# Asking for the copy of the turned shift rows two steps, not three, behind its transposing transfer

## The chip, the cores and the metric

One core of a Trainium2 chip runs the whole program. The metric is the device time of one execution in microseconds. A core has TensorE (matrix products), VectorE, ScalarE, GpSimd (POOL in the profile), and SyncE (SP), which here does nothing but issue transfers. The profile calls a transfer's issue by its queue, SPq for SyncE's.

## The reference

Three stages follow each other. Clustered attention lets a query attend only to keys of its own cluster; then comes a dense layer with a maximum over three products, and last a layer of eight experts. The change lies in the attention.

```python
q_assign = np.argmax(np.einsum('bhsd,hcd->bhsc', q_n, c_n), axis=-1)
k_assign = np.argmax(np.einsum('bhsd,hcd->bhsc', k_n, c_n), axis=-1)
mask = q_assign[:, :, :, None] == k_assign[:, :, None, :]
scores = np.where(mask, scale * np.matmul(q, k.transpose(0, 1, 3, 2)), -1000000000.0)
scores = scores - np.max(scores, axis=-1, keepdims=True)
attn = np.exp(scores)
attn = attn / (np.sum(attn, axis=-1, keepdims=True) + 1e-09)
attn_out = np.matmul(attn, v)                      # 2 batches, 8 heads, 768 rows, 64 wide
h = np.maximum(np.maximum(x @ w1, x @ w2), x @ w3) # x: 1536 rows of 512
x = h @ w_out
# then each row with x @ w_skip > 0 goes through one of 8 experts, weighted by its gate
```

## The kernel before

The 16 heads (two batches of eight) go through in pairs. This text numbers them 0 to 15; a pair holds an even head, called first, and an odd one, called second. A head takes six steps of the loop in `attention`, one for each tile of 128 keys, so there are 96 steps, and some before them to fill the pipeline. Each step asks every engine for a fixed list of instructions: two score products of two parts each (line 524, tiles Aq, Ak, Cq, Ck), the exponentials on ScalarE (line 527), the products with the values (line 565) of two steps before, and one step of the row maximum of a head that is up to eleven steps ahead (lines 465, 470 and 475).

The row maximum of a head has to be subtracted from its scores. The kernel does that inside the score product: the plane Aq holds, beside the query rows, 32 rows of shift values for each head. `shift` makes them when the head's sixth maximum is done: three small operations of GpSimd write the tile mq (lines 489 to 494), SyncE issues a transposing transfer from mq into a tile named pm (line 512), and later a second transfer copies 32 rows of pm into Aq (line 543). For heads 0 and 1 TensorE turns the rows instead, and ScalarE copies them. So the profile has 14 transposing transfers into pm and 14 copies out of it, in the order of heads 2 to 15. The first score product of a head (line 524) needs its copy.

`later(n, fn)` calls fn when the loop is n steps on, at the beginning of that step. What a step asks for is issued in the order of the calls, and each engine runs its own list in order. The transfers of SyncE thus stand in one list: a transfer whose source isn't there yet holds all that follow it. In that list stand also the loads of raw keys and queries (rawk, rawq, line 306), of the values (v, line 409) and of the dense layer's weights (wst and wsto, line 743), the copies of the key and query halves (Ak, Aq, Ck, Cq, lines 327 and 333), the transposed cluster rows (Mk, Mq, lines 512 and 543) and the transposed results (xh, xl, lines 611 and 615). The weights' loads have two buffers, and VectorE frees one when it has read it.

The copy's place is set by these lines; PW is a number in the table CF.

```python
M = self.turned(f"pm{nm}", mq.rearrange("p n j c -> p (n j c)"))
self.later(PW, lambda: self.copies()[AW[st["b"]]](Aq[r, j, :], M[r]))
```

AW is 2 for both batches, which picks SyncE's transfer as the copy.

Of the kernel before, what the change touches and what calls it, by code (L numbers as in the profile page):

```python
# [79 lines left out]
 'QS': 2,  # L80
 'QT': 6,
 'MW': [2, 0, 0],
 'PW': 3,
 'XS': 3,
 'XL': 1,
 'XR': [0, 1, 2],
# [1417 lines left out]
```

## Time and profile before

| | |
|---|---|
| time before, median of 3 executions | 526.34 us (525.97, 526.34 and 529.37) |
| the profiled execution | 530.19 us |
| its span, first to last instruction | 528.4 us |
| TensorE busy, products | 480.8 us (91%) |
| TensorE, loading of weights | 330.1 us (62%) |
| VectorE busy | 391.2 us (74%) |
| ScalarE busy | 314.0 us (59%) |
| GpSimd busy | 152.7 us (29%) |
| mean granted clock of TensorE | 0.970 |

Busy times come from one profiled execution. The loading of weights overlaps with the products. The granted clock is a share of TensorE's full speed. The attention's steps take the time from about 30 us to 320 us; up to about 145 us of it the attention runs nearly alone, and from there the dense layer's work is woven in.

### The profile page before, as it was taken

How to read it: one execution, taken by the hardware profiler on the slowest of the kernel's cores; microseconds unless marked ns; L12 is line 12 of the kernel's file. 1: busy time of each engine (PE TensorE's matmuls, PEld its weight loads, DVE VectorE, ACT ScalarE, POOL GpSimd, SP SyncE). 2: the span in 40 equal slices, each digit the busy share in tenths (PEclk: the TensorE clock that was granted, in tenths of full speed). 3: DMA queues.
4: the chain of work that ended last, by engine and by line, in shares of the span. 5: the costliest groups of instructions: out<-in, count | busy, mean ns of one | idle time of the engine just before them, and what ended most of it. 6: DMA issues, size and time to landing. Idle time of an engine off the chain costs nothing. (4 is left out here: it accounts for less than half of the span.)

```text
span 528.4 us, 11560 instructions
## 1 busy us (share of the span) xinstructions
PE 480.8 (91%) x4390; PEld 330.1 (62%) x4390; DVE 391.2 (74%) x828; ACT 314.0 (59%) x579; POOL 152.7 (29%) x197
## 2 busy tenths in 40 slices
PE   2689999899897989899999999999999999977993
PEld 1357777677775767566776766655656654445763
DVE  5656676645689899999999973344588867588992
ACT  5587777567676675656666654311556633465980
POOL 2424242422438344745375320000000000271112
PEclk9999999969998999989999999999999999989898
DMA  8649486935849427744534125316488854299970
GB/s 229 156 118 219 92 182 111 227 76 119 177 103 244 92 93 178 152 107 128 134 71 115 66 44 96 71 41 248 151 276 261 267 178 155 80 302 291 358 256 14
DMA packets 89836, 82.91 MB, mean 157 GB/s; under 512 B 55200, under 2 KB 72806, under 8 KB 89778
## 3 DMA queue, kind: packets, MB, share of 16 engines
q1 hardware_dynamic: 88082, 78.98, 55.5%
q0 software_dynamic: 976, 1.85, 1.7%
q10 hardware_dynamic: 720, 1.31, 0.7%
q8 instruction: 35, 0.57, 0.5%
q14 instruction: 23, 0.19, 0.1%
HBM read 57.18 MB, written 4.22 MB: 116 GB/s over the span
## 5 line engine op out<-in xcount | busy, mean ns | idle before, releaser
L527 ACT ACTIVATE p<-p 128x384 f32<-128x384 f32 x192 | 92.4, 492 | 53.4 <-PE p L524 48.5
L841 PE MATMUL h<-xh,wh 128*128 128x384 f16 x288 | 94.9, 330 | 1.8 <-DVE xl L604 1.8
L841 PE MATMUL h<-xh,wl 128*128 128x384 f16 x288 | 95.2, 330 | 0.0
L841 PE MATMUL h<-xl,wh 128*128 128x384 f16 x288 | 95.0, 330 | 0.0
L565 PEld LDWEIGHTS acc<-v,p 128*128 128x128 f32 x672 | 84.6, 197 | 9.1 <-issue 3.8
L565 PE MATMUL acc<-v,p 128*128 128x65 f32 x672 | 84.2, 276 | 0.3
L475 DVE CUSTOM_DVE_ANT_0 mh<-p,mh 128x384 f32<-128x384 f32 x96 | 52.9, 551 | 33.8 <-ACT mh L470 24.8
L841 PEld LDWEIGHTS <-wh 128*128 128x128 f16 x576 | 55.6, 100 | 35.5 <-DVE xl L604 1.9
L1108 DVE SCALAR_TENSOR_TENSOR e<-est,e 128x1024 f16<-128x1024 f32 x64 | 76.6, 1218 | 0.9 <-ACT e L1105 0.9
L524 PE MATMUL p<-Aq,Ak 128*128 128x384 f16 x192 | 64.7, 337 | 6.9 <-DMA Aq<-pm 3.4
L1105 ACT ACTIVATE e<-est 128x1024 f16<-128x1024 f32 x64 | 65.0, 1049 | 6.2 <-DMA est<-in_moe_w 5.6
L524 PE MATMUL p<-Cq,Ck 128*128 128x384 f16 x192 | 64.6, 336 | 0.0
L768 POOL TENSOR_TENSOR wma<-wma,wpw 128x512 f32<-128x512 f32 x24 | 31.3, 1306 | 66.4 <-DVE wma L767 44.2
L470 ACT ACTIVATE mh<-p 128x384 f32<-128x384 f32 x96 | 46.7, 487 | 2.8 <-PE p L465 2.4
L849 DVE TENSOR_TENSOR hm<-h,hm 128x384 f32<-128x384 f32 x48 | 26.6, 555 | 27.1 <-PE h L841 25.0
L854 ACT ACTIVATE hh<-hm 128x384 f16<-128x384 f32 x24 | 12.6, 523 | 55.7 <-DVE hm L849 55.7
L538 DVE TENSOR_TENSOR pl<-p,ph 128x768 f16<-128x768 f32 x40 | 42.5, 1062 | 2.6 <-ACT ph L537 2.6
L1147 POOL DMA_INDIRECT exe<-out,ixe x2 | 2.2, 1084 | 141.6 <-DVE me L1143 141.3
L841 PEld LDWEIGHTS <-wl 128*128 128x128 f16 x288 | 28.4, 99 | 19.2 <-issue 0.8
L465 PE MATMUL p<-Ak,Aq 128*128 128x384 f16 x96 | 33.7, 351 | 6.3 <-DVE mx L475 4.2
L465 PE MATMUL p<-D,Aq 128*128 128x384 f16 x96 | 33.9, 353 | 1.8 <-DVE D L338 1.6
L537 ACT ACTIVATE ph<-p 128x768 f16<-128x768 f32 x40 | 33.7, 844 | 1.3
(234 smaller groups left out, 916.0 us busy)
## 6 DMA issues: line engine op xcount, KB each, us to landing
est<-in_moe_w SPq DMA_DIRECT2D x64, 512.0 KB
wst<-in_moe_w SPq DMA_DIRECT2D x18, 512.0 KB
rawk<-in_kT SPq DMA_DIRECT2D x8, 384.0 KB
rawq<-in_qT SPq DMA_DIRECT2D x8, 384.0 KB
v<-in_vP SPq DMA_DIRECT2D x16, 192.0 KB
wsto<-in_moe_w_out SPq DMA_DIRECT2D x6, 512.0 KB
Ak<-Hk SPq DMA_DIRECT2D x16, 96.0 KB
Aq<-Hq SPq DMA_DIRECT2D x16, 96.0 KB
```

What stands on the lines that cost most here:

```text
L465: nc.tensor.matmul(pb[:, :384], lhsT=Aq[:, j, 128 * n:128 * n + 128], rhs=(st["D", j], Ak[:, j, 384:768])[u], start=True, stop=True)
L470: nc.scalar.activation(pbs[0], pb[:, :384], AF.Relu)
L475: nc.vector.tensor_tensor_reduce(pbs[0], pbs[1][:, :384], pbs[0], 1.0, -3.0e38, ALU.add, ALU.max, mx[:, n:n + 1])
L524: nc.tensor.matmul(pb[:, :384], lhsT=T["k"][:, j, ks], rhs=T["q"][:, j, 384 * u:384 * u + 384], start=first, stop=not first)
L527: nc.scalar.activation(p[:, u], pb[:, :384], AF.Exp, scale=2.0 ** -19)
L537: nc.scalar.activation(ph, p, AF.Copy)
L538: self.low_p = lambda: nc.vector.tensor_tensor(plo, p, ph, op=ALU.subtract)
L565: nc.tensor.matmul(o, lhsT=l, rhs=r, start=start, stop=stop, skip_group_check=True)
L768: nc.gpsimd.tensor_tensor(ma[i], ma[i], pw[i].bitcast(F32), op=ALU.mult)
L841: nc.tensor.matmul(ps[:, :384], lhsT=l, rhs=r[:, k, :], start=(k == 0 and i == 0), stop=(k == self.NK - 1 and i == 2))
L1105: nc.scalar.activation(hi, st, AF.Copy, scale=64.0)
L1108: nc.vector.scalar_tensor_tensor(lo, st, 64.0, hi, op0=ALU.mult, op1=ALU.subtract)
```

## The change

The number of steps between asking for the transposing transfer and asking for the copy goes from three to two. Nothing else is touched; every engine has the same instructions as before.

```diff
  'MW': [2, 0, 0],
- 'PW': 3,
+ 'PW': 2,
  'XS': 3,
```

On SyncE this moves the copy up in the list. Two places show it. The first is in the list of SyncE at the copy for head 4, the first head of its pair; Mk and Mq are the turned cluster rows of the next pair. Before:

```order
L512 DMA_TRANSPOSE pm_2_0_1261<-mq 128x6x128
L512 DMA_TRANSPOSE Mq_3_1297<-aq 128x6x128
L543 DMA Ak_3_1177<-Mk_3_1254 64x768 x2
L543 DMA Aq_3_1180<-Mq_3_1297 64x768 x2
L543 DMA Aq_2_674<-pm_2_0_1261 32x768
L327 DMA Ck_0_1488<-Lk_0_1380 64x768 x2
```

The same place of SyncE's list, with the change:

```order
L512 DMA_TRANSPOSE pm_2_0_1261<-mq 128x6x128
L512 DMA_TRANSPOSE Mq_3_1297<-aq 128x6x128
L543 DMA Ak_3_1177<-Mk_3_1254 64x768 x2
L543 DMA Aq_2_674<-pm_2_0_1261 32x768
L543 DMA Aq_3_1180<-Mq_3_1297 64x768 x2
```

The copy has changed places with the two copies of the next pair's turned query rows.

The second place is SyncE's list at the copy for head 5, the second head of the same pair; wst is a load of the dense layer's weights. Before:

```order
L512 DMA_TRANSPOSE pm_2_1_1498<-mq 128x6x128
L409 DMA v_3_1560<-in_vP 128x6x64 x2
L327 DMA Cq_0_1582<-Hq_0_1378 64x768 x2
L327 DMA Cq_0_1582<-Lq_0_1443 64x768 x2
L306 DMA rawk_1_1628<-in_kT 128x768
L306 DMA rawq_1_1630<-in_qT 128x768
L743 DMA wst_0_1633<-in_moe_w 128x4x256
L543 DMA Aq_2_674<-pm_2_1_1498 32x768
L611 DMA_TRANSPOSE xh_122<-x_1_1_1637 128x6x128
```

The same place of SyncE's list, with the change:

```order
L327 DMA Cq_0_1582<-Lq_0_1443 64x768 x2
L543 DMA Aq_2_674<-pm_2_1_1498 32x768
L306 DMA rawk_1_1629<-in_kT 128x768
L306 DMA rawq_1_1631<-in_qT 128x768
L743 DMA wst_0_1634<-in_moe_w 128x4x256
L611 DMA_TRANSPOSE xh_122<-x_1_1_1637 128x6x128
```

The copy now stands ahead of the loads of raw keys, raw queries and weights. For heads 3 and 7 it passes rawk and rawq alone. For head 11 it passes a load of weights alone, for head 14 a load of the last weights (wsto), and for heads 13 and 15 its place in SyncE's list stays as it was.

## Rows read from the trace of the kernel before

**Rows 1.** The page, busy time of each engine with its share of the span.
```profile
PE 480.8 (91%) x4390; PEld 330.1 (62%) x4390; DVE 391.2 (74%) x828; ACT 314.0 (59%) x579; POOL 152.7 (29%) x197
```

**Rows 2.** Waits from 60 to 320 us: us in total, times, longest.
```profile
PE p L465 <- DVE mx L475: 4.2, 4, 1.5
...
PE p L524 <- DMA Aq<-pm: 3.4, 2, 1.9
```

**Rows 3.** Timeline of TensorE at heads 4, 5, 7: start, us, instruction, idle before.
```profile
86.44 0.10 PEld L524 LDWEIGHTS <-Ak 128*128 128x128 f16 x1
...
102.56 0.34 PE L524 MATMUL p<-Aq,Ak 128*128 128x384 f16 x1 [1.95 <-DMA Aq<-pm]
...
136.40 0.34 PE L524 MATMUL p<-Aq,Ak 128*128 128x384 f16 x1 [1.48 <-DMA Aq<-pm]
```

**Rows 4.** Timeline of SyncE's issues, for heads 5, 7 and 15.
```profile
89.63 2.20 SPq L512 DMA_TRANSPOSE pm<-mq  x1
...
95.89 0.58 SPq L306 DMA_DIRECT2D rawk<-in_kT  x1
...
97.48 0.57 SPq L543 DMA_DIRECT2D Aq<-pm  x1
...
129.95 0.58 SPq L306 DMA_DIRECT2D rawk<-in_kT  x1
...
131.06 0.57 SPq L543 DMA_DIRECT2D Aq<-pm  x1
...
302.50 1.25 SPq L512 DMA_TRANSPOSE pm<-mq  x1
305.37 0.53 SPq L543 DMA_DIRECT2D Aq<-pm  x1
```

**Rows 5.** Timeline of SyncE's issues, for head 4.
```profile
77.48 1.89 SPq L512 DMA_TRANSPOSE pm<-mq  x1
...
80.80 1.23 SPq L543 DMA_DIRECT2D Ak<-Mk  x2
...
84.52 0.55 SPq L543 DMA_DIRECT2D Aq<-pm  x1
```

**Rows 6.** Waits of SyncE itself at line 543, whole span.
```profile
SPq L543 <- DMA Mq<-aq: 2.1, 4, 1.2
SPq L543 <- DMA pm<-mq: 1.6, 1, 1.6
```

**Rows 7.** Timelines of ScalarE and VectorE around 100 us.
```profile
99.99 0.52 ACT L527 ACTIVATE p<-p 128x384 f32<-128x384 f32 x1
103.09 0.49 ACT L527 ACTIVATE p<-p 128x384 f32<-128x384 f32 x1 [2.58 <-PE p L524]
...
101.08 0.55 DVE L475 CUSTOM_DVE_ANT_0 mh<-p,mh 128x384 f32<-128x384 f32 x1
```

**Rows 8.** Stretches: us, busy PE, PEld, DVE, ACT, POOL; PEclk, DMA, GB/s.
```profile
100.00:102.00 2.00, 0.61 (x19) 0.49 (x17) 1.64 (x4) 0.51 (x2) 1.05 (x2) 1.00 1.14 326
102.00:104.00 2.00, 1.44 (x10) 1.12 (x10) 0.00 (x1) 0.91 (x3) 1.84 (x4) 0.92 1.12 239
104.00:112.00 8.00, 8.00 (x38) 6.56 (x38) 2.44 (x8) 3.18 (x6) 3.36 (x5) 0.50 1.00 138
112.00:114.00 2.00, 2.00 (x9) 1.45 (x8) 1.97 (x5) 1.62 (x4) 0.65 (x1) 0.52 0.31 76
...
134.00:137.00 3.00, 1.52 (x25) 1.08 (x23) 1.95 (x6) 0.89 (x4) 1.66 (x3) 1.00 1.21 136
```

**Rows 9.** Timeline of TensorE: last products of heads 1, 3, 5 and 7.
```profile
63.30 0.35 PE L565 MATMUL acc<-vs,Aq 32*128 32x65 f16 x6
...
91.52 0.35 PE L565 MATMUL acc<-vs,Aq 32*128 32x65 f16 x6
...
125.88 0.36 PE L565 MATMUL acc<-vs,Aq 32*128 32x65 f16 x6
...
155.00 0.35 PE L565 MATMUL acc<-vs,Aq 32*128 32x65 f16 x6
```

## The prediction

> **What bounds the kernel now.** I read the busy shares first, then the waits of TensorE, then the queue of SyncE around those waits, and last the granted clock. TensorE is busy for 91% of the span [rows 1]. So the kernel is as long as TensorE's fixed list of instructions plus the holes in it, and a hole that is closed early moves all the later work forward, since each engine's instructions stand in a fixed order and the later loads are asked for by the same steps. The list of waits names few holes. One of them is the copy of this change: TensorE waits twice for the transfer of the shift rows into the query plane (the tile Aq, from pm), 3.4 us in total [rows 2]. The two places are the first score product of head 5, at 102.56 us after 1.95 us of idling, and of head 7, at 136.40 us after 1.48 us [rows 3]. The other twelve copies landed before TensorE was there or cost it almost nothing.
>
> The queue tells why these two. SyncE issued the transposing transfer of head 5 at 89.63 us and the copy out of its result only at 97.48, behind the loads of the next raw keys and queries and a load of weights (rawk, rawq, wst; 384, 384 and 512 KB), which took its place from 95.89 on; for head 7 the copy went out at 131.06, behind rawk and rawq from 129.95 on [rows 4]. From issue to the product it took 102.56 - 97.48 = 5.08 us and 136.40 - 131.06 = 5.34 us. A copy of head 4, which has no big loads ahead of it, was issued at 84.52 [rows 5], and TensorE loaded weights for that head's first product at 86.44 [rows 3]: at most 1.92 us. So the copy is late for two reasons: it is asked for late, and it rides behind big loads.
>
> **The change part by part.** Nothing is added or removed; a copy moves up one step, past what SyncE issues in that step. There are two kinds of place.
>
> *Second head of a pair (heads 3, 5, 7, 9 and 11).* The copy moves ahead of rawk, rawq or a load of weights, or all of them. Head 5's copy takes rawk's place, 95.89, and head 7's takes 129.95. What does its landing become? Both ends come from rows: at best 1.92 us after issue (97.81 and 131.87), at worst as long as before (95.89 + 5.08 = 100.97 and 129.95 + 5.34 = 135.29), since the four copies Cq and the values v still stand ahead. TensorE would have been ready at 102.56 - 1.95 = 100.61 and at 136.40 - 1.48 = 134.92. The rest of the wait is 0 to 0.36 us at head 5 and 0 to 0.37 at head 7. The gain is 1.59 to 1.95 plus 1.11 to 1.48, together 2.7 to 3.4 us. I take 3.4: what made 5.1 out of 1.9 must be mostly the megabyte that no longer stands ahead.
>
> *First head of a pair (heads 2, 4, 6, ...).* The copy now stands between Ak<-Mk and Aq<-Mq (heads 2 to 12). TensorE waited for none of these, so the gain is nought. The cost could be that SyncE stands at the copy until the transposition lands. The copy's new place in head 4's pair is 80.80 + 1.23 = 82.03 us, 4.55 us after its transposition was issued [rows 5]. The one transposition whose landing SyncE did wait for, at 302.50 us, was followed by its copy 2.87 us later [rows 4], and SyncE's waits list that single wait, of 1.6 us [rows 6]. So the new place comes late enough, and I take nought; behind the copy stand the two Aq<-Mq, which wait for a transposition issued later anyway. Were that cover gone, they would be later by the missing time plus the copy's own 0.55 us of issue.
>
> *What is moved past.* rawk, rawq and wst go out 0.57 us later, the issue time of the copy [rows 4]. The waits of 60 to 320 us, of which two stand in [rows 2], hold none of any engine for these three. So nought again, and at most 0.57 us a pair if the cover were gone.
>
> *What is late next.* At head 5, ScalarE had ended its last exponential at 99.99 + 0.52 = 100.51 and then sat idle 2.58 us waiting for TensorE; VectorE's row maximum of that step ended at about 101.6 [rows 7]. TensorE's next need of ScalarE was thus met 0.1 us before 100.61, and it needs that maximum's bank only in the next step. Nothing takes the wait's place at once.
>
> *The sum.* Against the profiled execution (530.19 us: a span of 528.4 and 1.8 us around it): 530.19 - 3.4 = 526.8 us. Against the median, 526.34 - 3.4 = 522.9 us.
>
> **The clock.** There is a second price on head 5's wait. After it the granted clock fell: 1.00 in 100 to 102 us, 0.92 in 102 to 104, 0.50 in 104 to 112, 0.52 in 112 to 114 [rows 8]: the lower of two levels (1.2 against 2.4 GHz) for about 0.3 + 8 + 1.9 = 10.2 us. Head 7's shorter wait left the clock at 1.00 [rows 8]. What did it cost? The last products of a head mark a period. Two heads take 91.52 - 63.30 = 28.22 us before, 155.00 - 125.88 = 29.12 after, which holds the wait of 1.48 (so 27.64), and 125.88 - 91.52 = 34.36 over the slow stretch, which holds the wait of 1.95 [rows 9]. The excess is 34.36 - 1.95 - 28.22 = 4.2 to 34.36 - 1.95 - 27.64 = 4.8 us; I use 4.5. In the profiled execution this goes too if the wait goes: 526.8 - 4.5 = 522.3. But the profiled execution is 3.85 us above the median, and of the three times two lie at 526 and one at 529.37. A slow stretch of 4.5 us that comes in some executions and not in others would explain that split. So I hold it likelier that the median execution had the wait without the fall of the clock, and has only 3.4 us to win.
>
> The Trainium skill ("TensorE: Matmul & The Clock Gate", section "HAM oscillation — how this bites in real kernels") prices a slow stretch at its length times one half. By that it would be worth 10.2 x 0.5 = 5.1 us, and the rival below with the clock would end 0.6 us lower; the periods say 4.2 to 4.8, and the sum goes by them.
>
> **The rivals.** *The clock comes back too:* the median execution had the slow stretch like the profiled one, and without the wait it doesn't come. 526.34 - 3.4 - 4.5 = 518.4 us. For it speaks that the clock fell right behind the longest wait; against it that one of two waits had no such effect, and that the profile is slower than the median. *The wait is given back:* the copy lands early, but TensorE, now up to 3.4 us ahead, meets another hole: the list has waits for VectorE's maximum, 4.2 us in four [rows 2]. If they grow by what is won, the time stays at 526.3. Against it speaks that VectorE and ScalarE idle in the stretch of the two waits [rows 7]. The same time comes out if the copy lands no sooner in spite of its new place, but the bound above leaves that only 0.7 us. *Slower:* SyncE stands at the copy in its new place, because under load the transposition takes longer than the 4.55 us that separate them. SyncE's longest wait of that kind, for another transposition (Mq), is 1.2 us [rows 6]. At the seven first heads this is up to 8.4 us of a stopped queue; if the keys and queries behind it passed all of it on to TensorE, 526.34 - 3.4 + 8.4 = 531.3 us. It decides from a landing later than 4.55 us after issue, for which no row speaks.
>
> **How the numbers follow.** The waits alone go: 522.9, chance 0.50. The clock too: 518.4, 0.25. Given back: 526.3, 0.17. Slower: 531.3, 0.08. The forecast is 522.9. The range leaves out the slower case and the lower part of the clock's: 518.0 to 526.8. One per cent is 5.3 us, about what a measurement of this kernel can tell from no change. Faster by more than that needs less than 521.1: nearly all of the clock's case (0.24) and a fifth or so of the first, where a part of the slow stretch goes as well (0.11), together 0.35. Slower by that much, above 531.6, is the upper half of the last case and what I may have overlooked: 0.06. Within one per cent: 0.59.
>
> **What would show it.** Right: in the waits of TensorE the entry for this copy shrinks from 3.4 us to below 0.8; the copies of heads 5 and 7 leave SyncE ahead of rawk; two heads take about 28 us also between the marks that now lie 34.36 apart. The clock of that stretch shows whether the second price is gone, and a fall elsewhere that it has moved. Wrong: SyncE's wait for the transposition grows well over 1.6 us (the slower rival), or TensorE's waits for VectorE or ScalarE grow by about 3 us between 100 and 300 us (given back). What would break the forecast most is the clock, since it costs more than both waits and doesn't follow from the order of instructions.

## The result, and the profile after

The changed kernel takes 521.76 us in the median of six executions (516.35 to 525.84); before takes 526.63 us, also of six (524.96 to 529.37). The ratio is 0.9888, with a 95% interval of 0.9842 to 0.9933. The profiled execution took 519.58 us, with a span of 517.8 us. A repetition on another chip, told below, gives 521.41 against 527.01 us.

The ratios leave out executions more than 1.5% above the fastest of their kernel, for before 13 of 29 in the second set below and 10 of 23 in the third, so that a ratio there tends to understate a gain, and the medians of all executions stand beside it.

The list of waits from 60 to 320 us, of the changed kernel (us in total, times, longest us), no longer has TensorE's entry for the copy that [rows 2] show:

```profile
PE p L465 <- DVE mx L475: 5.3, 6, 1.5
...
PE h L841 <- DVE xl L604: 2.5, 1, 2.5
...
PE p L524 <- ACT p L527: 1.6, 5, 0.5
```

The timeline of TensorE shows the first score products of heads 5 and 7 without idle time before them, where [rows 3] had 1.95 and 1.48 us, and the last products of heads 1, 3, 5 and 7, as in [rows 9], and of head 15:

```profile
62.19 0.35 PE L565 MATMUL acc<-vs,Aq 32*128 32x65 f16 x6
...
90.16 0.35 PE L565 MATMUL acc<-vs,Aq 32*128 32x65 f16 x6
...
99.04 0.33 PE L524 MATMUL p<-Aq,Ak 128*128 128x384 f16 x1
...
117.81 0.35 PE L565 MATMUL acc<-vs,Aq 32*128 32x65 f16 x6
...
126.70 0.33 PE L524 MATMUL p<-Aq,Ak 128*128 128x384 f16 x1
...
145.28 0.36 PE L565 MATMUL acc<-vs,Aq 32*128 32x65 f16 x6
...
330.87 0.35 PE L565 MATMUL acc<-vs,Aq 32*128 32x65 f16 x6
```

Two heads now take 27.97, 27.65 and 27.47 us; before they took 28.22, 34.36 and 29.12. From the mark of head 1 to that of head 7 the profiled executions differ by 91.70 - 83.09 = 8.6 us, of a difference in span of 528.4 - 517.8 = 10.6. So four fifths of the difference lie in these three pairs. Of the 8.6 us, 3.4 are the two waits, and most of the rest is the slow stretch behind head 5, which this execution of before had and another one (below) had not.

SyncE's timeline shows where the copies went (compare [rows 4, 5]); the first three rows are head 4's, the next three head 5's, the last two head 7's:

```profile
79.44 1.28 SPq L543 DMA_DIRECT2D Ak<-Mk  x2
80.83 0.56 SPq L543 DMA_DIRECT2D Aq<-pm  x1
82.03 1.11 SPq L543 DMA_DIRECT2D Aq<-Mq  x2
...
94.47 0.56 SPq L543 DMA_DIRECT2D Aq<-pm  x1
95.08 0.58 SPq L306 DMA_DIRECT2D rawk<-in_kT  x1
...
96.23 0.38 SPq L743 DMA_DIRECT2D wst<-in_moe_w  x1
...
122.15 0.56 SPq L543 DMA_DIRECT2D Aq<-pm  x1
122.76 0.58 SPq L306 DMA_DIRECT2D rawk<-in_kT  x1
```

Head 5's copy went out 4.57 us before the product that needs it, head 7's 4.55 us, and neither held TensorE. The list of transfers (KB each, median us from issue to landing) shows that the fourteen copies were not all as quick as the 1.92 us of the prediction's better end:

```profile
Aq<-pm SPq DMA_DIRECT2D x14, 48.0 KB, 3.3
```

SyncE's own waits at line 543 for the transposition are 2.4 us in two, at heads 14 and 15, against one of 1.6 before [rows 6]:

```profile
SPq L543 <- DMA pm<-mq: 2.4, 2, 1.5
```

The granted clock (PEclk, the third number from the end, ahead of DMA share and GB/s) stays at 1.00 behind head 5, where [rows 8] had 0.50. The one fall of the clock in the attention came later, behind a stretch in which TensorE was busy for 2.06 us of 5:

```profile
100.00:102.00 2.00, 2.00 (x19) 1.74 (x18) 1.41 (x5) 0.82 (x3) 1.80 (x3) 1.00 1.20 204
102.00:110.00 8.00, 8.00 (x80) 6.57 (x78) 5.12 (x14) 7.09 (x15) 3.06 (x6) 1.00 1.09 164
...
155.00:160.00 5.00, 2.06 (x26) 1.42 (x26) 4.97 (x11) 1.61 (x4) 3.58 (x5) 0.97 1.01 287
160.00:164.00 4.00, 4.00 (x19) 2.25 (x17) 3.96 (x6) 2.58 (x6) 3.32 (x4) 0.61 1.02 167
```

It isn't head 5's fall in a new place: before had a fall of the same length there, about 3.4 us at the lower level, beside the one behind head 5. Before:

```profile
165.00:168.00 3.00, 1.01 (x20) 0.78 (x20) 3.00 (x7) 1.37 (x3) 2.01 (x3) 1.00 1.06 294
168.00:172.00 4.00, 4.00 (x16) 1.90 (x15) 4.00 (x7) 1.30 (x3) 3.57 (x4) 0.57 0.87 203
```

### The profile page after: what moved, and what is told of

Its sections match the earlier page's. It is cut to its first block, busy times and chain, and to the rows that moved or that the text cites. A ratio compares the mean times of both kernels' runs of the same rounds, so it can differ in the third digit from the quotient of the medians.

```text
span 517.8 us, 11568 instructions
## 1 busy us (share of the span) xinstructions
PE 470.1 (91%) x4390; PEld 324.3 (63%) x4390; DVE 393.6 (76%) x828; ACT 313.5 (61%) x579; POOL 154.7 (30%) x197
## 5 line engine op out<-in xcount | busy, mean ns | idle before, releaser
L565 PEld LDWEIGHTS acc<-v,p 128*128 128x128 f32 x672 | 81.7, 192 | 9.6 <-issue 4.4
L565 PE MATMUL acc<-v,p 128*128 128x65 f32 x672 | 81.7, 271 | 0.2
L524 PE MATMUL p<-Aq,Ak 128*128 128x384 f16 x192 | 63.0, 328 | 3.9 <-ACT p L527 1.8
L524 PE MATMUL p<-Cq,Ck 128*128 128x384 f16 x192 | 62.8, 327 | 0.0
L538 DVE TENSOR_TENSOR pl<-p,ph 128x768 f16<-128x768 f32 x40 | 44.0, 1101 | 2.6 <-ACT ph L537 2.6
L465 PE MATMUL p<-Ak,Aq 128*128 128x384 f16 x96 | 32.5, 339 | 8.1 <-DVE mx L475 5.3
L465 PE MATMUL p<-D,Aq 128*128 128x384 f16 x96 | 32.7, 341 | 1.8 <-DVE D L338 1.6
```

The lines of the kernel that those rows point to most:

```text
L465: nc.tensor.matmul(pb[:, :384], lhsT=Aq[:, j, 128 * n:128 * n + 128], rhs=(st["D", j], Ak[:, j, 384:768])[u], start=True, stop=True)
L524: nc.tensor.matmul(pb[:, :384], lhsT=T["k"][:, j, ks], rhs=T["q"][:, j, 384 * u:384 * u + 384], start=first, stop=not first)
L538: self.low_p = lambda: nc.vector.tensor_tensor(plo, p, ph, op=ALU.subtract)
L565: nc.tensor.matmul(o, lhsT=l, rhs=r, start=start, stop=stop, skip_group_check=True)
```

## The experiments

The theory: the gain is the copy of heads 5 and 7 that no longer stands behind the big loads in SyncE's list; its price is the two waits and, in executions where the clock falls behind head 5's wait, that fall. The rivals: the first heads' copies have a part, the number of steps matters and not the order, or the gain is chance in the clock. Three sets ran, each on one chip with its own executions of before: 27 (median 527.94 us, mean granted clock 0.9757), 29 (526.51 us, 0.9787) and 23 (527.01 us, 0.9771).

### First set: which copies, and is it the order?

**Second heads alone.** The copies of heads 3, 5, 7, 9, 11, 13 and 15 two steps behind, the others three.

```diff
- self.later(PW, lambda: ...
+ self.later(PW - j, lambda: ...
```

> Only the second heads of the pairs (3, 5, 7, 9, 11) get the copy two steps behind; the first heads keep three. My theory (the gain is the copy put ahead of the raw loads at heads 5 and 7): like the changed kernel, no wait of TensorE for this copy above 0.4 us in total, granted clock 1.00 behind head 5, ratio to before 0.985 to 0.993. Rival (the first heads' earlier copy has a part in it, since SyncE's list is shorter by one transfer ahead of the next pair): a ratio above 0.995 with some of the wait left. Rival (all of it is chance in the clock): the waits go, but the ratio is 0.993, the 3.4 us alone.

Measured: 522.64 us, ratio 0.990 (0.9863 to 0.9937). TensorE's waits for the copies shrink to one, at the first score product of head 8, a first head:

```profile
143.22 0.34 PE L524 MATMUL p<-Aq,Ak 128*128 128x384 f16 x1 [0.34 <-DMA Aq<-pm]
```

So the second heads carry the gain. The first heads' copy is not quite free to stay: with TensorE earlier, head 8's becomes the late one, by 0.34 us, which the full change doesn't show.

**First heads alone.**

```diff
- self.later(PW, lambda: ...
+ self.later(PW - 1 + j, lambda: ...
```

> Only the first heads (2, 4, ..., 14) get the copy two steps behind; the second heads keep three. My theory: nothing changes, waits of 1.5 to 2 us at heads 5 and 7 stay, 3 to 4 us in total, ratio 0.997 to 1.003. Rival (first heads matter): the waits shrink, ratio below 0.995.

Measured: 527.73 us, ratio 1.001 (0.9984 to 1.0035). TensorE's waits for the copies, from 40 to 320 us, stay:

```profile
PE p L524 <- DMA Aq<-pm: 4.3, 2, 2.8
```

They are 2.8 us at head 5 and 1.5 at head 7. As expected, nothing is won.

**Three steps, but the raw loads asked for one step later.** The copy keeps its steps; rawk and rawq move behind it.

```diff
- CF = {'T': {'qk': -33,
+ CF = {'T': {'qk': -32,
```

> The copy stays three steps behind, but the loads of raw keys and queries are asked for one step later, so that they stand behind the copy in SyncE's list; at head 5 the load of weights still stands ahead of it. My theory (the order in SyncE's list is what matters, the number of steps is nothing by itself): the wait at head 7 is gone, the one at head 5 is below 1.2 us (0.5 MB ahead instead of 1.3), total wait below 1.3 us, ratio 0.985 to 0.995. Rival (the copy has to be asked for earlier): the waits stay at 3 to 4 us, ratio 0.997 to 1.003.

Measured: 524.65 us, ratio 0.9921 (0.9883 to 0.996). Head 7's wait is gone, head 5's is 0.32 us. In total I was wrong: the waits sum up to 2.6 us, since two first heads now wait, head 4 for 1.48 and head 8 for 0.79 us. Waits of 40 to 320 us, and the timeline of TensorE at head 4:

```profile
PE p L524 <- DMA Aq<-pm: 2.6, 3, 1.5
```

```profile
88.78 0.34 PE L524 MATMUL p<-Aq,Ak 128*128 128x384 f16 x1 [1.48 <-DMA Aq<-pm]
```

These two copies were not slow once issued: they took 1.92 us (86.86 to 88.78) and 1.95 us (143.16 to 145.11) from issue to product, about the 1.92 that head 4's took at most in before. They were issued late: counted from the last product of head 1, head 4's copy went out after 86.86 - 64.18 = 22.68 us, against 84.52 - 63.30 = 21.22 in before. The moved loads now stand in SyncE's list ahead of head 4's transposition, which likely makes the delay; no run separates it. ScalarE, too, waited 0.5 and 0.3 us for raw keys and queries here. At the second heads it is the order in SyncE's list that makes the copy late, since the steps are those of before. By the waits, moving the small copy up is better than moving the big loads down, 0.3 us against 2.6; the times point the same way, 522.64 against 524.65 us, but the intervals of the ratios overlap.

**Four steps.**

```diff
- 'PW': 3,
+ 'PW': 4,
```

> The copy is asked for four steps behind: at heads 3, 5 and 7 it then stands behind the transposed result xh and the four copies of the key and query halves as well. My theory: TensorE waits 3 to 5 us at each of the three heads, 10 to 14 us in total, and the granted clock falls to 0.50 behind most of these waits, each time for 1.5 to 5 us of loss; time 10 to 25 us above before, ratio 1.02 to 1.05. Rival (the clock has nothing to do with these waits): the waits alone, ratio 1.012 to 1.02, and the falls of the clock stand elsewhere.

Measured: 548.29 us, ratio 1.0406 (1.0359 to 1.0453). TensorE waits at heads 3, 5, 7, 9 and 11:

```profile
PE p L524 <- DMA Aq<-pm: 16.3, 5, 4.8
```

I had expected waits at three heads and 10 to 14 us. The clock fell behind four of the five waits, for about 3.4 us behind heads 3 and 11 and for almost 14 us each behind heads 5 and 7, where half of it, about 7 us, is more than the 5 I had allowed; the stretches before and after the two products, same columns as above:

```profile
100.00:108.00 8.00, 5.12 (x64) 3.92 (x62) 6.16 (x14) 5.11 (x11) 4.19 (x5) 1.00 1.02 256
108.00:122.00 14.00, 11.94 (x52) 9.11 (x53) 3.86 (x11) 5.27 (x11) 4.86 (x8) 0.51 0.52 105
140.00:145.00 5.00, 3.08 (x37) 2.40 (x35) 4.12 (x9) 3.10 (x8) 3.08 (x3) 1.00 1.08 220
145.00:160.00 15.00, 12.95 (x59) 10.13 (x59) 4.61 (x14) 5.66 (x11) 3.29 (x8) 0.54 0.47 99
```

The waits grew by 16.3 - 3.4 to 4.3, some 12 to 13 us, the median by 20.35 us. The mean granted clock over the executions was 0.9528 against 0.9757. A share of the clock missing over a span is time lost: 0.0472 x 547.1 = 25.8 us (mean span) against 0.0243 x 526.6 = 12.8 us. The two together, 12.5 + 13, overshoot the 20.35 us by 5, so the two do not simply add up here; a part of waits or of slow clock may be hidden beside other engines' work, but these runs don't show it.

### Second set: heads 5 and 7 apart, one step, and before again

**Head 5 alone.**

```diff
- self.later(PW, lambda: ...
+ self.later(PW - (st["b"] == 0 and st["hp"] == 2 and j == 1), lambda: ...
```

> Only head 5's copy is two steps behind its transposition; the thirteen others keep three. My theory (head 5's wait costs its 2 to 2.8 us, and on top the fall of the clock that follows it in many executions): head 5's wait gone, head 7's 1.5 us left, clock 1.00 behind head 5, ratio 0.990 to 0.995. Rival (the clock falls somewhere anyway, whatever the waits): the ratio is 0.995 to 0.997, the wait alone.

Measured: 524.32 us against 526.51, ratio 0.9964 (0.9918 to 1.0009). Waits of 40 to 320 us:

```profile
PE p L524 <- DMA Aq<-pm: 1.7, 1, 1.7
```

That is head 7's. The mean granted clock was 0.9821 against 0.9787. The ratio is not in my range but in the rival's (0.995 to 0.997); its interval holds both, so this run alone does not decide between them.

**Head 7 alone.** The same with `st["hp"] == 3`.

> Only head 7's copy is two steps behind its transposition. My theory (a wait of 1.5 us, seldom followed by a fall of the clock): head 7's wait gone, head 5's of 2 to 2.8 us left with a fall of the clock behind it, ratio 0.996 to 0.999. Rival (the change works as a whole, each copy the same share): as much as with head 5 alone, 0.990 to 0.995.

Measured: 525.78 us, ratio 0.9982 (0.9939 to 1.0025); mean granted clock 0.9772. Waits of 40 to 320 us, 2.3 us at head 5 and 0.4 at head 8:

```profile
PE p L524 <- DMA Aq<-pm: 2.7, 2, 2.3
```

By the medians head 5 is worth 2.2 us and head 7 0.7; both intervals hold 1, and they overlap, so the sizes are not told apart by the times. The profiles do show each wait removed by its own copy. And in this profile the clock did not fall behind head 5's wait of 2.3 us, which I had expected it to.

**One step.**

```diff
- 'PW': 3,
+ 'PW': 1,
```

> The copy one step behind the transposition instead of two. At a second head it then stands ahead of the values and of Cq, right behind the transposition, so that SyncE has to wait for its landing. My theory (nothing is left to win at these copies, and the transposition lands 2.9 to 3.5 us after issue): SyncE waits for the transposition at most copies, 1 to 2 us each, 10 to 20 us in total; TensorE waits for no copy; time as with two steps, ratio 0.985 to 0.993. Rival (slower: the held queue makes the keys and queries behind it late): TensorE or the exponentials wait for those transfers, ratio above 0.997.

Measured: 520.26 us against 526.51, ratio 0.9946 (0.9903 to 0.999); mean granted clock 0.9806. No wait of TensorE for a copy. SyncE's own waits at the copies:

```profile
SPq L543 <- DMA pm<-mq: 14.3, 13, 1.6
```

SyncE now stands 13 times, for 1.1 us each, until the transposition has landed. The copies behind it are quick, 1.9 us in the median from issue to landing where the change has 3.3:

```profile
Aq<-pm SPq DMA_DIRECT2D x14, 48.0 KB, 1.9
```

That is the mechanism of my slower rival, at a size of 14.3 us in all, and it costs nothing that the times show. The ratio lies between my range and the rival's, and the medians make 0.988. The held queue is felt elsewhere: GpSimd waits longer for the values. Waits of 40 to 320 us, in this run, in the changed kernel of the third set and in one step of the third set:

```profile
POOL v L413 <- DMA v<-in_vP: 18.7, 4, 6.8
...
POOL v L413 <- DMA v<-in_vP: 14.0, 5, 4.5
...
POOL v L413 <- DMA v<-in_vP: 20.2, 4, 6.1
```

**Before, once more with a profile.** Its line numbers are one higher.

> The kernel before, once more with a profile. My theory (the fall of the clock behind head 5's wait comes in some executions and with different lengths): waits at heads 5 and 7 again, 3 to 4.5 us in total; the slow stretch behind head 5 may be missing or shorter than the 10.2 us of the first profile, and the time then nearer to 526 than to 530 us. Rival (the fall always comes with that wait): the same 10 us of half clock, time about 530.

Measured: 526.42 us. The waits are there, 2.6 us at head 5 and 1.6 at head 7, and the clock did not fall behind them. Waits from 40 to 320 us, and the stretch from 95 to 130 us with its granted clock of 1.00:

```profile
PE p L525 <- DMA Aq<-pm: 4.2, 2, 2.6
```

```profile
95.00:130.00 35.00, 31.84 (x352) 25.47 (x350) 23.25 (x58) 26.32 (x57) 13.35 (x18) 1.00 0.82 167
```

So the fall behind head 5 comes in some executions and not in others, with the same wait.

### Third set: a long wait put back, and the two best side by side

**The changed kernel with head 5's copy four steps behind.**

```diff
- self.later(PW, lambda: ...
+ self.later(PW + 2 * (st["b"] == 0 and st["hp"] == 2 and j == 1), lambda: ...
```

> The changed kernel, but head 5's copy alone is asked for four steps behind its transposition. My theory (a long wait brings the fall of the clock, one and the same mechanism behind the profile of before): TensorE waits 4 to 5.5 us at head 5 and nowhere else for a copy, and in the profile the granted clock stands at 0.50 behind it for 3 to 14 us; time 6 to 10 us above the kernel with two steps everywhere, half of it or less beyond the wait. Rival (the falls of the clock have other causes): the wait's 4 to 5.5 us alone, no fall between 100 and 125 us.

Measured: 529.40 us, ratio to before 1.0115 (1.0014 to 1.0215), 8.0 us above the changed kernel of the same set. Waits of 40 to 320 us, and the stretch around head 5:

```profile
PE p L524 <- DMA Aq<-pm: 4.3, 1, 4.3
```

```profile
95.00:130.00 35.00, 30.25 (x317) 24.05 (x315) 20.48 (x51) 23.10 (x50) 12.25 (x18) 0.95 0.59 137
```

One wait of 4.3 us costs 8.0 us. 0.95 over 35 us is about 3.5 us at the lower level in this execution; over all six the mean clock was 0.9730 against 0.9816 of the changed kernel, 0.0270 x 528.5 - 0.0184 x 519.6 = 14.3 - 9.6 = 4.7 us. The wait and the clock's loss make 9.0 us, near the 8.0 between the medians and the 530.26 - 521.39 = 8.9 between the means.

**Two steps and one step on the same chip.**

> The changed kernel, once more beside before: no wait for the copies in the profile, mean granted clock over its executions above that of before, ratio 0.985 to 0.993. Rival (the first ratio was a lucky draw of the clock): 0.993 to 0.998.

Measured: 521.41 us, ratio 0.9927 (0.9889 to 0.9965), mean granted clock 0.9816 against 0.9771 of before. Its profile has no wait for a copy either. The ratio is at the upper end of my range, and its interval reaches into the rival's; the medians make 0.989.

> One step behind, on the same chip as two steps. My theory (nothing left to win at the copies, SyncE's held time is hidden): the two within 0.4% of each other. Rival (one step is better, since second heads' copies land 3 us sooner still): lower than two steps by more than 0.4%.

Measured: 522.49 us, ratio 0.9958 (0.9917 to 0.9998), mean granted clock 0.9816. One step and two steps are 0.2% apart here and were 520.26 and 521.41 in two different sets: not told apart. No version was shown to be faster than the change.

## Why the prediction came out as it did

The time forecast was 522.9 us, the measured median 521.76, and the ratio 0.9888 lies 1.1% below before, at the edge of what I had called telling: just beyond one per cent, for which I had given 0.35, and not within it (0.59), though its interval reaches to both sides. The gain forecast was 3.4 us; measured are 4.9 between the medians here and 5.6 in the third set. The time came out closer than the gain, and what is missing from the gain is the clock's term below.

**What bounds the kernel.** Right: a hole in TensorE's list that closes early moves the rest forward. The marks of the heads show it. From head 7's mark to that of the last head, head 15, it is 340.21 - 155.00 = 185.2 us before and 330.87 - 145.28 = 185.6 after: what was won by head 7 was kept. (Before has two short falls of the clock in that stretch, after one, so this holds to about 2 us.) Head 15's mark in before:

```profile
340.21 0.35 PE L565 MATMUL acc<-vs,Aq 32*128 32x65 f16 x6
```

**The second heads.** Right, with the better end of the gain: both waits went entirely, not to 0.36 us. That needs a landing within 100.61 - 95.89 = 4.72 and 134.92 - 129.95 = 4.97 us of the issue, not the 1.92 at the better end of the bound. That the megabyte ahead made most of the 5.1 out of 1.9 is not shown: with the loads behind them the copies took 3.3 us in the median, and 1.9 in the run at one step, where they go out right behind the transposition. The runs tell the cause apart: second heads alone give 0.990, first heads alone 1.001, and the order without the step removes the same two waits but for 0.32 us.

**The first heads.** Nought was right for the change, as the run with them alone shows. I had not seen that the first heads have next to no slack: head 8 waits in the run with the second heads alone, where TensorE is ahead, and heads 4 and 8 in the run with the loads later, where their copies go out later. In the changed kernel their earlier copies cover this, worth some 0.3 us. The one first head at which SyncE now stands is head 14, for 2.4 - 1.5 = 0.9 us, and TensorE doesn't wait for it.

**What is moved past.** Right. No engine waits for rawk, rawq or wst.

**What is late next.** Right at the place I looked at. TensorE's waits for VectorE's maximum went from 4.2 us in four to 5.3 in six, which looks like a part given back; but before, profiled again, has 5.1 in six, so that is within the spread of executions.

**The clock: the term that was mis-sized.** I read it as a yes or no of the median execution and took no. It is a share: of six profiles with a wait at head 5 above 1.9 us the clock fell behind it in four (10.2 us in the first profile of before, 3.4 with first heads alone, nearly 14 at four steps, 3.4 with the wait put back) and stayed in two (before again, head 7 alone). In the seven profiles that have no such wait, or one of 0.3 us, it fell between 95 and 130 us in none. The price therefore comes as a mean over executions. In the third set the mean clock gives 0.0229 x 524.9 - 0.0184 x 519.6 = 12.0 - 9.6 = 2.4 us. The means of the times, 526.71 and 521.39 us, differ by 5.3 us; that leaves 2.9 us for the waits, of which the profiles show 3.4 to 4.2. So I estimate the true sum at about 3 + 2.4 where mine was 3.4 + 0; of the 4.5 us of the case "the clock comes back too", about half came back on average. The mean clock is that of the whole span, and it doesn't say which falls went. That head 5's wait has to do with it is borne out by the second set: with head 5's wait gone the mean clock was 0.9821, with only head 7's gone 0.9772, twelve executions each on one chip, a difference of 0.005 with a 95% interval of about 0.004 to either side. Why the clock falls in one execution and not in another stays open.

**The slower rival.** It was to decide from a landing later than the copy's place, and in the change SyncE waits for one twice, 1.5 us at the longest. The run at one step forced the condition, with SyncE held 14.3 us, and it still wasn't slower. The second half of that rival, the held time being passed on to TensorE, is what fails: GpSimd waited longer, TensorE did not.

The page of the Trainium skill on the clock ("TensorE: Matmul & The Clock Gate", "HAM oscillation — how this bites in real kernels") prices a slow stretch at half its length. Reckoning lost time as the missing share of the clock is the same rule, and the run with one wait put back bears it out within 1 us (9.0 reckoned, 8.0 measured), while at four steps it overshoots by 5 us.

## What to carry to other kernels

In a list of transfers that is issued in order, look at what stands directly ahead of a small transfer on which the busiest engine waits: here, behind 0.8 to 1.3 MB of loads that nobody needed for several steps, a small transfer took 5.1 to 5.3 us from its issue to the product that waited for it; with the loads behind it, such copies took 3.3 us in the median. Move the small one ahead of them rather than the big ones back: with the loads moved back, other copies were issued late. And price a wait of TensorE in the mean over executions, with the clock's share: waits of 3.4 to 4.3 us were worth 5 to 9 us here.

## What the runs showed of the hardware

The granted clock falls behind the same wait in one execution and not in another (before: 10.2 us at the lower level behind 1.95 us of idling, and none behind 2.6 us). Falls of the clock, these and others, go with much of the spread of this kernel on one core: before went from 519.39 to 533.73 us in 29 executions of one chip, with mean clocks from 0.966 to 0.989, and the correlation between the time and the time lost by the clock (its missing share of the span) is 0.82.

Holding SyncE was cheaper than I had thought: 13 waits of 1.1 us at the head of the list, in a stretch with more than a hundred transfers, did not delay TensorE, though GpSimd waited 18.7 us for the values where it waits 14.0 in the changed kernel of the third set.
